# Weighted sums of an attention kernel as eight 64x32 TensorE tiles with two PSUM banks, and the single row maxima taken out of the main steps

## Chip, core and metric

The kernel runs on one core of one Trainium2 chip. The metric is the device time of one execution in microseconds (us): the median of the runs, 1456.09 us for the kernel before (2 runs, 1455.58 to 1456.61).

## What is computed

The reference mixes two attention branches of the same 2048 rows of x (512 wide) with a gate. All data are float32.

```python
x = A_x                                            # 2048 x 512
g = sigmoid((x * gate_w).sum(-1, keepdims=True))
# branch A: 32 heads of 16; each row sees 8 keys, 0, 2, ..., 14 rows back
# branch B: 32 query heads of 16, one key head and one value head for all of them
q = (x @ wq)  as 32 heads;  k = x @ wk;  v = x @ wv        # k, v: 2048 x 16
p = softmax(q k^T / 4);     o = p v                        # every row sees all 2048 keys
return g * a + (1 - g) * (o @ wo_b)
```

Branch B is the big part: 32 heads x 2048 queries x 2048 keys of scores, their exponentials, and the weighted sums of v.

## The kernel before, in words

**Units and steps.** Branch B is cut into 32 units: 4 blocks of 512 queries times 8 groups of 4 heads. A unit goes through 16 steps, one for each tile of 128 keys; all 512 steps stand in one loop (`for s in range(NS + 1)`). `kt` is the step's number in its unit. A step has these parts:

- `exp_pair(s, 0)` and `exp_pair(s, 1)` (L471, L477): TensorE computes two heads' scores of 128 keys x 512 queries into the two halves of a PSUM tile `pe0` or `pe1` (two matmuls that use the upper and the lower 64 rows of the array), and ScalarE writes their exponentials to an SBUF tile `pexp`.
- `weighted(s - 1)` (L486): the step before's `pexp` times `vst`, the values of the key tile (128 keys x 32 columns, of which 17 matter: 16 values and a column of ones, whose sum is the softmax's denominator). Head i of four goes to partitions 32i to 32i+31 of one PSUM bank, `po`, so four matmuls with 128x32 tiles of the array stand side by side. They add up over the 16 steps of a unit. These operands are full float32, and the profile shows each such matmul as two.
- Row maxima. The softmax needs each query's largest score ahead of its exponentials. They are found for units that come later, in 2048 pieces of 128 queries x 512 keys: TensorE computes the scores once more (L328), VectorE reduces them into `mx`. A **pair** (`fill_pair`, L350) does two pieces at once in a two-bank PSUM tile `pm`. A **single** (`fill_one`, L362) does one piece in the bank `m1`, which the profile calls `ps`. In the stages with other matmuls, `fill_diff` and `fill_sum` (L399, L411, L423) do two pieces with ScalarE's help.

When all 64 pieces of a unit are there, a chain makes two extra rows of that unit's query tile `qst` of them: L338 and L340 on VectorE, `mh` (L441) on ScalarE, `ml` (L447, L448) on GpSimd, eight small DMAs `qst<-ml` (L459). The unit's first score matmul waits for them.

**The order.** Each engine works its queue in program order. The program is written by a planner that runs at build time: it keeps clocks for the engines with fixed costs, and decides in each step which parts go in. `singles(s)` spreads singles over the steps so that the maxima are ready in time. Where a unit's maxima would come too late, `pause(n)` writes n pieces in a row, as pairs that take turns in `pe0`, `pm` and `pe1`, with no exponentials between them; the kernel before has no such pause.

**Unit end.** At a unit's end (`kt == 0` of the next) `finish_a` turns `po` on VectorE (L500), takes the reciprocals of the sums (L506), and GpSimd scales the result; the next unit's first weighted sum overwrites `po` and so waits for L500.

**Other stages.** Up to about 280 us the projections run (L1110, with maxima in between). GpSimd does branch A beside the main steps. Three times an output phase (`out_phase`, L804) computes four row groups of the output; there `m1` and `po` serve for maxima as well once the unit's sum has left `po`. The last rows of the output follow after step 511 (L1322, L1352); L1332 is the last unit's transpose.

Of the kernel before, what the change touches and what calls it, by code (L numbers as in the profile page):

```python
# [6 lines left out]
F32 = mybir.dt.float32  # L7
# [6 lines left out]
P = 128  # L14
S = 2048
D = 512
# [32 lines left out]
def gated_mix_kernel(ctx, tc, xt, wa, wk, wq, wo_a, wo_b, out):  # L49
# [280 lines left out]
    def to_go():  # L330
        return 2 * len(slots) + len(half)
# [151 lines left out]
    def weighted(s):  # L483
        u, kt = divmod(s, NJ)
        for i in (3, 2, 1, 0):
            nc.tensor.matmul(po[32 * i:32 * i + 32, :], vst[:, kt, :], pexp[s, i // 2][:, i % 2, :], start=(kt == 0), stop=(kt == NJ - 1))  # L486
        del pexp[s, 0], pexp[s, 1]
        after("pe", exped.pop(s) + 0.1, T_W)

# [7 lines left out]

    def finish_a(u, eng):
        tt = pe[0].tile([P, 4 * 4, 32], F32, name="tt", bufs=1)
        nc.vector.transpose(tt.rearrange("p b d -> p (b d)"), po)  # L500
        finish_b(u, tt, eng)

    def finish_b(u, tt, eng):
# [120 lines left out]
            woh.append(p2b[0].tile([P, C, D], F32R, name=f"woh{k}"))  # L624
            wol.append(p2b[0].tile([P, C, D], F32R, name=f"wol{k}"))

    wot = {}

    def wo_load(k, c):
        wot[k, c] = p2b[0].tile([P, 512], F32, name="os", tag="two", bufs=1)  # L630
# [2 lines left out]
    def wo_split(k, c):  # L633
        t = wot.pop((k, c))
        split(woh[k][:, c, :], wol[k][:, c, :], t, nc.gpsimd)

    turned, later = {}, {}

# [41 lines left out]
    def out_store(j, k, closing):  # L680
        nonlocal pool
        del turned[j, 0], turned[j, 1]
        two = p2b[0].tile([P, 2, D], F32, name="two", bufs=1)
        if closing:
            nc.scalar.activation(two[:, 0], eb[k][:, 0, :], AF.Copy)
            other = p2b[0].tile([P, D], F32, name="other", bufs=1)
            nc.vector.tensor_copy(other, eb[k][:, 1, :])  # L687
            free[f"e{k}"] = max(after("act", clk["pe"] + T_LAT, 0.5), after("dve", clk["pe"] + T_LAT, 0.66))
        else:
            nc.scalar.activation(two, eb[k], AF.Copy)  # L690
            free[f"e{k}"] = after("act", clk["pe"] + T_LAT, 0.92)
        pool = max(pool, 1e3 * free[f"e{k}"]) + 1300
        nc.gpsimd.tensor_add(two[:, 0], two[:, 0], other if closing else two[:, 1])
        nc.sync.dma_start(out[0].rearrange("(p j) d -> p j d", j=NJ)[:, j, :], two[:, 0])
# [47 lines left out]
    def stream(seq, mm, done, s):  # L742

        nonlocal pp2
        at, told = [0, 0], 0
        ready = free.pop("m2")
        pp2.release()
        pp2 = tc.alloc_tile_pool(name="parts", bufs=1, space=PSUM)
        if len(held[0]) < 2:
            more = p1x[0].tile([P, 2, 512], F32, name="dd2", tag="qx", bufs=1)  # L750
            for b in range(2):
                held[b].append(more[:, b])
                read_d[b].append(0.0)
        apart[:] = [pp2.tile([P, 512], F32, name=f"pd{k}") for k in range(2)]
        free["d0"] = free["d1"] = ready
        free["po"] = 1e9
        cl = [clk["pe"]] * 2
        while min(at) < len(seq) or any(pend):
            if free["po"] > 1e8 and min(at) > 3 and max(cl) > exped[s - 1] + 0.1:
                clk["pe"] = max(cl)  # L760
                weighted(s - 1)
                finish_a((s - 1) // NJ, nc.gpsimd)
                free["po"] = clk["dve"] + 0.1
                cl = [clk["pe"]] * 2
            if apart and max(at) > len(seq) - 10 and s in exped and max(free["d0"], free["d1"]) <= max(cl):
                clk["pe"] = max(cl)
                rejoin()
                exp_pair(s, 1, m2, "m2")
                cl = [clk["pe"]] * 2
            b = int(cl[1] < cl[0])  # L770
            clk["pe"] = cl[b]
            do = side_fill(b, max(at) > len(seq) - 10)
            if do:
                do()
                cl[b] += T_R
            elif at[b] < len(seq) and at[b] <= at[1 - b] + 2:
                dur = mm(b, seq[at[b]])
                cl[b] = clk["pe"] + dur
                at[b] += 1
            else:  # L780
                cl[b] += 0.07
            clk["pe"] = cl[b]
            while told < min(at):
                told += 1
                done(seq[told - 1])
        plain_todo()
        clk["pe"] = max(cl)
        if apart:
            rejoin()
            exp_pair(s, 1, m2, "m2")  # L790
# [79 lines left out]

    def singles(s):

        steps = 16 * (NU - 1) - 8 - s
        if steps <= 0 or to_go() <= 0:
            return to_go() > 0
        owing[0] += (to_go() - 1.94 * steps - 15.5 * (NJ - 4 - outs)) / steps
        owing[0] = min(owing[0], 3.0)
        if s % 16 == 1:
            return True
        if s % 16 == 0 or owing[0] < 1.0 or clk["dve"] - clk["pe"] > 1.5 and owing[0] < 2.0:  # L880
            return False
        return True

    def fill_ready(key, slack):
        if fillable() and free[key] <= clk["pe"] + slack:
# [375 lines left out]
    for s in range(NS + 1):  # L1261
# [18 lines left out]
        if outs == NJ - 4:  # L1280
            if short > 0 and steps < 2:
                pause(short)
        elif due or outs < NJ and outs // NH in done and kt == 15 and NHG * (k + 1) - 1 in shaped and (lead < LEAD or s >= 16 * (NHG * (k + 2) + 1) - 1):
# [44 lines left out]
    for x in range(2):  # L1328
        js = slice(2 * x, 2 * x + 2)
        two = four[:, x]  # L1330
        tt, own = two[:, 0].rearrange("p (b d) -> p b d", d=32), two[:, 1]
        nc.vector.transpose(two[:, 0], po[:, 256 * x:256 * x + 256])  # L1332
        rl = wp.tile([P, 8], F32, name="rll", tag="rl", bufs=2)
        nc.vector.reciprocal(rl, tt[:, :, 16])
        rv = rl.rearrange("p (j b) -> p j b", b=4)
        nc.vector.tensor_mul(rv, rv, gate_t[:, :, NJ - 4 + 2 * x:NJ - 2 + 2 * x].rearrange("p b j -> p j b"))
        nc.vector.tensor_mul(obp["t"][:, 8 * x:8 * x + 8, 1, :], tt[:, :, 0:DH], rl.unsqueeze(2).to_broadcast([P, 8, DH]))
        nc.vector.transpose(own, obp["t"][:, 8 * x:8 * x + 8].rearrange("p b h d -> p (b h d)"))
        tl = wp.tile([P, 2, 256], F32R, name=f"tl{x}", tag="aext", bufs=2)
# [53 lines left out]
```

## Time and profile before

| what | value |
|---|---|
| median of the runs | 1456.09 us |
| span of the profiled execution, first to last instruction | 1454.0 us |
| around the span (1456.09 - 1454.0) | 2.1 us |
| main steps with output phases | 282.4 us (first weighted sum) to 1432.5 us |
| granted TensorE clock | 1.00 throughout |

The profile's own execution has no time outside of its span, so the 2.1 us are the median's distance to it. The span is a sum of stages: projections to 280 us, then 512 steps, of which three hold an output phase of about 33 us, then some 21 us of last rows. Busy shares are means over all of them; what one step costs is read from the timeline.

### The profile page before, as it was taken

To read this page: it belongs to the slowest core of one execution; us is meant where nothing else is said; L and a number is where in the kernel's file an instruction comes from. 1 tells how busy PE (TensorE), PEld (TensorE's weight loads), DVE (VectorE), ACT (ScalarE), POOL (GpSimd) and SP (SyncE) were. 2 spreads that over 40 slices of the span, in tenths; PEclk is the share of its full clock that TensorE was granted. 3 is DMA by queue.
4 is the path that set the end of the run, shared out by engine and by line. 5 is a ranking of instruction groups with operands and counts; after the bars stand their busy time and mean duration, and the time that the engine had idled before them with its cause. 6 is when DMAs were issued, how large, how long until landed. Compare 5 with 4: busy or idle time off the path is not lost.

```text
span 1454.0 us, 29596 instructions
## 1 busy us (share of the span) xinstructions
PE 1445.0 (99%) x10989; PEld 744.9 (51%) x10989; DVE 1144.9 (79%) x1851; ACT 1289.6 (89%) x1643; POOL 955.1 (66%) x1716
## 2 busy tenths in 40 slices
PE   9999999999999999999999999999999999999999
PEld 6899999833333333333333373333333743373335
DVE  6888888788787888888888877888788778778821
ACT  5888888799999999999999979999999889879994
POOL 5941888888979898888898897988981211130000
PEclk9999999999999999999999999999999999999999
DMA  6652442411202102012022020211200000000000
GB/s 226 169 172 75 138 144 75 135 49 42 80 17 74 64 27 69 31 39 79 19 73 72 13 94 16 75 43 42 72 12 13 27 16 1 2 31 1 1 2 29
DMA packets 45688, 85.70 MB, mean 59 GB/s; under 512 B 10400, under 2 KB 28248, under 8 KB 41448
## 3 DMA queue, kind: packets, MB, share of 16 engines
q1 hardware_dynamic: 38552, 45.21, 10.1%
q0 software_dynamic: 6560, 37.95, 7.8%
q8 instruction: 86, 1.41, 0.4%
q10 hardware_dynamic: 432, 0.66, 0.1%
q14 instruction: 58, 0.48, 0.1%
HBM read 57.97 MB, written 25.25 MB: 57 GB/s over the span
## 4 chain that ended last, share of the span: by engine, by line
PE 96%; DVE 1%; ACT 1%; DMA 0%; issue 0%; POOL 0%; SPq 0%; ACTq 0%; DVEq 0%
PE po L486 34%; PE pe L471 25%; PE pf L1110 12%; PE pm L328 8%; PE ps L328 5%; PE pe L804 4%; PE pd L399 3%; PE po L328 1%; PE pe L1322 1%; PE pf L195 1%; ACT pexp L477 1%; DVE mx L350 1%; DMA xraw<-xt 0%; PE pm L862 0%; PE pe L652 0%
## 5 line engine op out<-in xcount | busy, mean ns | idle before, releaser
L477 ACT ACTIVATE pexp<-pe 128x1024 f32<-128x1024 f32 x1021 | 984.2, 1023 | 66.2 <-PE pe L471 61.9
L350 DVE TENSOR_REDUCE mx<-pm 128x2 f32<-128x1024 f32 x474 | 579.1, 1222 | 172.3 <-PE pm L328 168.9
L486 PE MATMUL po<-pexp,vst 128*32 128x512 f32 x4096 | 545.5, 605 | 0.0
L471 PE MATMUL pe<-qst,kst 64*128 64x512 f32 x1914 | 494.4, 458 | 3.3 <-DVE other L687 3.1
L471 PEld LDWEIGHTS pe<-qst,kst 64*128 64x128 f32 x1914 | 194.8, 183 | 437.5 <-ACT pexp L477 408.0
L411 ACT ACTIVATE dd<-pd 128x512 f32<-128x512 f32 x378 | 221.3, 602 | 50.6 <-PE pd L399 24.9
L362 DVE TENSOR_REDUCE mx<-ps 128x1 f32<-128x512 f32 x313 | 212.6, 679 | 4.4 <-PE pe L804 3.0
L328 PE MATMUL ps<-kst,qst 62*128 62x512 f32 x476 | 194.0, 408 | 0.1
L549 POOL TENSOR_TENSOR pr<-aext 128x256 f32<-128x256 f32 x256 | 182.0, 739 | 4.3 <-DMA aext<-ad 4.0
L328 PE MATMUL pm<-kst,qst 62*128 62x512 f32 x886 | 179.8, 398 | 0.3
L609 POOL TENSOR_TENSOR oa<-oa,av 128x256 f32<-128x256 f32 x224 | 164.2, 733 | 15.7
L486 PEld LDWEIGHTS po<-pexp,vst 128*32 128x32 f32 x4096 | 80.6, 108 | 167.8 <-issue 159.0
L423 DVE CUSTOM_DVE_ANT_0 dd<-ps,dd 128x512 f32<-128x512 f32 x190 | 130.9, 689 | 26.2 <-PE ps L328 10.5
L1110 PE MATMUL pf<-wah,xl 64*128 64x384 f32 (+1 forms) x496 | 149.2, 337 | 0.0
L606 POOL TENSOR_TENSOR av<-aext,lg 128x256 f32<-128x256 f32 x224 | 139.4, 622 | 12.8
L1110 PE MATMUL pf<-wah,xh 64*128 64x384 f32 (+1 forms) x496 | 147.4, 337 | 0.0
L1110 PE MATMUL pf<-wal,xh 64*128 64x384 f32 (+1 forms) x496 | 146.7, 337 | 0.0
L399 PE MATMUL pd<-kd,qst 62*128 62x512 f32 x366 | 144.3, 398 | 0.0
L423 DVE CUSTOM_DVE_ANT_0 dd<-po,dd 128x512 f32<-128x512 f32 x188 | 129.6, 690 | 17.9 <-PE po L328 8.8
L328 PEld LDWEIGHTS ps<-kst,qst 62*128 62x128 f32 x476 | 88.0, 185 | 33.0 <-DVE mx L362 27.1
L513 POOL TENSOR_TENSOR rl<-rl,gate_t 128x16 f32<-128x16 f32 x31 | 7.1, 230 | 136.6 <-DVE rl L506 136.5
L1110 PEld LDWEIGHTS pf<-wah,xl 64*128 64x128 f32 x496 | 91.1, 186 | 0.1
(211 smaller groups left out, 1816.1 us busy)
## 6 DMA issues: line engine op xcount, KB each, us to landing
aext<-ad POOLq DMA_DIRECT2D x32, 1056.0 KB, 5.5
ad<-stage SPq DMA_DIRECT2D x32, 384.0 KB
qst<-qd SPq DMA_DIRECT2D x60, 128.0 KB
xraw<-xt SPq DMA_DIRECT2D x16, 256.0 KB
qd<-qhi SPq DMA_DIRECT2D x16, 256.0 KB
qd<-qlo SPq DMA_DIRECT2D x16, 256.0 KB
qst<-qd SPq DMA_DIRECT2D x60, 64.0 KB
qst<-ml SPq DMA_DIRECT2D x212, 2.0 KB
```

The costliest lines, as they stand in the source:

```text
L328: nc.tensor.matmul(dst, qst[place(v)][b:b + 62, pr, t * P:(t + 1) * P], kst[b:b + 62, kc * 512:(kc + 1) * 512], start=True, stop=True)
L350: got = nc.vector.tensor_reduce(m[:, :, pr, t, kc], dst, AX.X, ALU.max)
L362: got = nc.vector.tensor_reduce(m[:, odd, pr, t, kc:kc + 1], dst, AX.X, ALU.max)
L399: nc.tensor.matmul(dst, qst[place(v)][b:b + 62, pr, t * P:(t + 1) * P], kd[0][b:b + 62, kc // 2, :], start=True, stop=True)
L411: got = nc.scalar.activation(held[b][k], dst, AF.Relu)
L423: got = nc.vector.tensor_tensor_reduce(held[b][k], dst, held[b][k], 1.0, -FMAX, ALU.add, ALU.max, m[:, b, pr, t, kc:kc + 1])
L471: nc.tensor.matmul(bank[:, odd, :], kst[b:b + 64, kt * P:(kt + 1) * P], qst[place(u)][b:b + 64, pr, :], start=True, stop=True)
L477: got = nc.scalar.activation(e, bank, AF.Exp, scale=SCALE)
L486: nc.tensor.matmul(po[32 * i:32 * i + 32, :], vst[:, kt, :], pexp[s, i // 2][:, i % 2, :], start=(kt == 0), stop=(kt == NJ - 1))
L549: nc.gpsimd.tensor_mul(pr[:, k], q, e[:, o:o + NH, AC:2 * AC])
L609: nc.gpsimd.tensor_add(ao, ao, av)
L1110: inst = nc.tensor.matmul(home(x)[0][:, :n], l[h], r[h], start=(i == 0 and b == 0), stop=(i == 3 * C - 1 and b == 1))
```

## The change

The weighted sum uses eight 64x32 tiles: keys 0 to 63 of a tile go to the bank `m1` (`ps`), keys 64 to 127 to `po`. At a unit's end ScalarE copies `m1` to a new SBUF tile `both`, VectorE adds `po`, and the transpose reads `both`. As `m1` is now taken during a unit, `singles` always says no. In an output phase `m1` is free for maxima only once the sum has left it. An output phase begins only when all of its weights are split. (Lines that only give a tile its tag or keep the list of splits are left out.)

```diff
     def weighted(s):
         u, kt = divmod(s, NJ)
         for i in (3, 2, 1, 0):
-            nc.tensor.matmul(po[32 * i:32 * i + 32, :], vst[:, kt, :], pexp[s, i // 2][:, i % 2, :], start=(kt == 0), stop=(kt == NJ - 1))
+            for b, bank in enumerate((m1, po)):
+                h = slice(64 * b, 64 * b + 64)
+                nc.tensor.matmul(bank[32 * i:32 * i + 32, :], vst[h, kt, :], pexp[s, i // 2][h, i % 2, :], start=(kt == 0), stop=(kt == NJ - 1))
...
     def finish_a(u, eng):
         tt = pe[0].tile([P, 4 * 4, 32], F32, name="tt", bufs=1)
-        nc.vector.transpose(tt.rearrange("p b d -> p (b d)"), po)
+        both = p2b[0].tile([P, 512], F32, name="both", tag="other", bufs=1)
+        nc.scalar.activation(both, m1, AF.Copy)
+        nc.vector.tensor_add(both, both, po)
+        nc.vector.transpose(tt.rearrange("p b d -> p (b d)"), both)
         finish_b(u, tt, eng)
...
-        free["po"] = 1e9
+        free["po"] = free["m1"] = 1e9
...
-                free["po"] = clk["dve"] + 0.1
+                free["po"] = free["m1"] = clk["dve"] + 0.1
...
     def singles(s):
 
-        steps = 16 * (NU - 1) - 8 - s
-        if steps <= 0 or to_go() <= 0:
-            return to_go() > 0
-        owing[0] += (to_go() - 1.94 * steps - 15.5 * (NJ - 4 - outs)) / steps
-        owing[0] = min(owing[0], 3.0)
-        if s % 16 == 1:
-            return True
-        if s % 16 == 0 or owing[0] < 1.0 or clk["dve"] - clk["pe"] > 1.5 and owing[0] < 2.0:
-            return False
-        return True
+        return False
...
-        elif due or outs < NJ and outs // NH in done and kt == 15 and ...
+        elif due or outs < NJ and not wot and len(split_done) == 2 * C and outs // NH in done and kt == 15 and ...
...
-        nc.vector.transpose(two[:, 0], po[:, 256 * x:256 * x + 256])
+        hs = slice(256 * x, 256 * x + 256)
+        if x == 0:
+            both = p2b[0].tile([P, 512], F32, name="both", tag="other", bufs=1)
+            nc.scalar.activation(both, m1, AF.Copy)
+            nc.vector.tensor_add(both, both, po)
+        nc.vector.transpose(two[:, 0], both[:, hs])
```

From here on the changed file's line numbers differ by a few: its weighted matmul is L488, its copy L503, its add L504, its transpose L505, its reciprocal L511.

**TensorE, an ordinary step** (step 359, `kt` 7 of unit 22). `pe_4203` and `pe_4204` are `pe0` and `pe1`; `ps` is the bank `m1`; `qst` with a number is a unit's query tile; `x2` means two equal rows. Before:

```order
L471 MATMUL pe_4203<-qst_80,kst 128x512 x2
L328 MATMUL pm<-kst,qst_82 128x512
L328 MATMUL ps<-kst,qst_76 128x512
L471 MATMUL pe_4204<-qst_80,kst 128x512 x2
L486 MATMUL po<-pexp,vst 32x512 x4
```

Now:

```order
L471 MATMUL pe_4203<-qst_80,kst 128x512 x2
L328 MATMUL pm<-kst,qst_81 128x512 x2
L471 MATMUL pe_4204<-qst_80,kst 128x512 x2
L488 MATMUL ps<-pexp,vst 32x512
L488 MATMUL po<-pexp,vst 32x512
L488 MATMUL ps<-pexp,vst 32x512
L488 MATMUL po<-pexp,vst 32x512
```

(The last two rows come twice more.) The single into `ps` is gone, and the four weighted matmuls are eight. Over the program the reductions of `ps` to one maximum go from 313 to 9. The query tile of the maxima is a sign of how far ahead they are: `qst_82` and `qst_76` belong to units 24 and 25 before, `qst_81` to unit 23 now, the very next one.

**TensorE, the next step** (step 360, `kt` 8 of unit 22). Before, it is the step above without the `ps` row. Now 17 pairs stand ahead of its exponentials, in turns of `pe_4203`, `pm` and `pe_4204`; these are the last four of them and what follows:

```order
L328 MATMUL pm<-kst,qst_81 128x512 x2
L328 MATMUL pe_4204<-kst,qst_81 128x512 x2
L328 MATMUL pe_4203<-kst,qst_81 128x512 x2
L328 MATMUL pm<-kst,qst_81 128x512 x2
L471 MATMUL pe_4203<-qst_80,kst 128x512 x2
L471 MATMUL pe_4204<-qst_80,kst 128x512 x2
L488 MATMUL ps<-pexp,vst 32x512
```

This is a pause. The program has 11 of them, at `kt` 8 of units 16, 20 to 24 and 26 to 30, with 159 pairs in all (10, 9 and 3 pairs at units 16, 20 and 26, and 17 or 18 at the other eight). Pairs in `pe0` and `pe1` go from 0 to 104, pairs in `pm` from 474 to 522. In the unit of a pause, `mh` of the next unit stands 4 steps ahead of that next unit on ScalarE (5 at the first pause); before, the shortest distance was 6 steps.

**VectorE at a unit's end.** Before:

```order
L340 STREAM_TRANSPOSE mt<-ms 128x32
L500 STREAM_TRANSPOSE tt<-po 128x512
L506 RECIPROCAL rl<-tt 128x16
L350 TENSOR_REDUCE mx<-pm 128x2
L362 TENSOR_REDUCE mx<-ps 128x1
```

Now:

```order
L504 TENSOR_TENSOR both<-both,po 128x512
L505 STREAM_TRANSPOSE tt<-both 128x512
L511 RECIPROCAL rl<-tt 128x16
L350 TENSOR_REDUCE mx<-pm 128x2 x2
L338 TENSOR_REDUCE ms<-mx 128x32
```

The add stands ahead of the transpose, and the next step's pair reduction behind all three. The copy that the add waits for stands on ScalarE behind the exponentials of the step in which the unit ends, and ahead of the next step's:

```order
L477 ACTIVATE pexp<-pe_4203 128x1024
L477 ACTIVATE pexp<-pe_4204 128x1024
L503 ACTIVATE both<-ps 128x512
L477 ACTIVATE pexp<-pe_4203 128x1024
L477 ACTIVATE pexp<-pe_4204 128x1024
```

Copy and add are there 31 times in the loop and once in the last rows. The output phases stand in steps 272, 288 and 400; before, in 272, 400 and 448.

More of the change, by code (lines that the diff above doesn't have):

```diff
@@ L625, in phase2 @@
             wol.append(p2b[0].tile([P, C, D], F32R, name=f"wol{k}"))
-    wot = {}
+    wot, split_done = {}, []
     def wo_load(k, c):
@@ L635, in wo_split @@
         split(woh[k][:, c, :], wol[k][:, c, :], t, nc.gpsimd)
+        split_done.append((k, c))
     turned, later = {}, {}
@@ L685, in out_store @@
             nc.scalar.activation(two[:, 0], eb[k][:, 0, :], AF.Copy)
-            other = p2b[0].tile([P, D], F32, name="other", bufs=1)
+            other = p2b[0].tile([P, D], F32, name="other", tag="other", bufs=1)
             nc.vector.tensor_copy(other, eb[k][:, 1, :])
@@ L1282, in gated_mix_kernel @@
                 pause(short)
-        elif due or outs < NJ and outs // NH in done and kt == 15 and NHG * (k + 1) - 1 in shaped and (lead < LEAD or s >= 16 * (NHG * (k + 2) + 1) - 1):
+        elif due or outs < NJ and not wot and len(split_done) == 2 * C and outs // NH in done and kt == 15 and NHG * (k + 1) - 1 in shaped and (lead < LEAD or s >= 16 * (NHG * (k + 2) + 1) - 1):
             if not due:
```

## Prediction

> **What bounds the kernel now.** I read the page first (busy shares and the chain of waits), then the timeline of two ordinary steps, then a unit's end.
>
> ```profile
> span 1454.0 us, 29596 instructions
> PE 1445.0 (99%) x10989; PEld 744.9 (51%) x10989; DVE 1144.9 (79%) x1851; ACT 1289.6 (89%) x1643; POOL 955.1 (66%) x1716
> PE 96%; DVE 1%; ACT 1%; DMA 0%; issue 0%; POOL 0%; SPq 0%; ACTq 0%; DVEq 0%
> ```
>
> TensorE holds 96% of the chain: nothing that it waits for is long, so what it issues, it pays for. ScalarE is next. The timeline of two steps shows how near it is (columns: start, length, engine, line, operation, shape, count):
>
> ```profile
> 699.46 1.94 ACT L477 ACTIVATE pexp<-pe 128x1024 f32<-128x1024 f32 x2 [0.19 <-PE pe L471]
> 699.69 1.23 DVE L350 TENSOR_REDUCE mx<-pm 128x2 f32<-128x1024 f32 x1
> 700.09 0.16 PEld L486 LDWEIGHTS po<-pexp,vst 128*32 128x32 f32 x8 [0.36 <-issue]
> 700.09 1.06 PE L486 MATMUL po<-pexp,vst 128*32 128x512 f32 x8
> 700.83 0.68 DVE L362 TENSOR_REDUCE mx<-ps 128x1 f32<-128x512 f32 x1
> 701.09 0.50 PE L471 MATMUL pe<-qst,kst 64*128 64x512 f32 x2
> 701.43 0.40 PE L328 MATMUL pm<-kst,qst 62*128 62x512 f32 x2
> 701.66 0.39 PE L471 MATMUL pe<-qst,kst 64*128 64x512 f32 x2
> 701.99 1.06 PE L486 MATMUL po<-pexp,vst 128*32 128x512 f32 x8
> ...
> 703.55 0.40 PE L328 MATMUL ps<-kst,qst 62*128 62x512 f32 x1
> 703.63 0.56 PE L471 MATMUL pe<-qst,kst 64*128 64x512 f32 x2
> ...
> 704.12 1.06 PE L486 MATMUL po<-pexp,vst 128*32 128x512 f32 x8
> ```
>
> From weighted sum to weighted sum a step without a single takes 701.99 - 700.09 = 1.90 us, one with a single 704.12 - 701.99 = 2.13 us: the single costs 0.23 us of TensorE, the distance at which matmuls of 512 columns follow each other (701.43 to 701.66). ScalarE's two exponentials fill 1.94 us; one alone takes 1.02 (row below), so the second starts 0.92 after the first, and a step cannot be shorter than 2 x 0.92 = 1.84 us whatever TensorE does. VectorE's pair reduction makes room for the next one after 700.83 - 699.69 = 1.14 us, well below a step.
>
> **The change, part by part.** The rows for the prices:
>
> ```profile
> L477 ACT ACTIVATE pexp<-pe 128x1024 f32<-128x1024 f32 x1021 | 984.2, 1023 | 66.2 <-PE pe L471 61.9 <-DVE mx L423 0.9
> L350 DVE TENSOR_REDUCE mx<-pm 128x2 f32<-128x1024 f32 x474 | 579.1, 1222 | 172.3 <-PE pm L328 168.9
> L486 PE MATMUL po<-pexp,vst 128*32 128x512 f32 x4096 | 545.5, 605 | 0.0
> L411 ACT ACTIVATE dd<-pd 128x512 f32<-128x512 f32 x378 | 221.3, 602 | 50.6 <-PE pd L399 24.9 <-DVE mx L423 13.3 <-PE pf L1110 2.1
> L663 DVE TENSOR_TENSOR qst<-pe,qst 128x512 fp32r<-128x512 f32 x12 | 8.2, 685 | 0.0
> ```
>
> *1. Singles out.* 313 become 9: 304 x 0.23 = **-70 us**. Hidden behind nothing, since TensorE is the bound of the step.
>
> *2. Their pieces come back in the pauses.* 159 pairs stand in 11 pauses. There TensorE has three places (`pe0`, `pm`, `pe1`), each free only when VectorE has read it, so VectorE sets the pace: 1.14 us a pair by the timeline, at most the 1.22 of the group's mean. No exponential can run beside them, since `pe0` and `pe1` hold maxima, so ScalarE's work cannot hide them. The next exponential needs the last turn but one, so a pause of n pairs holds the step up by n - 1 reductions: 159 - 11 = 148 x 1.14 = **+169 us** (to 148 x 1.22 = 181). The steps with a pause save their own pair, 11 x 0.23 = 2.5 us, which I leave for the start of each pause (a matmul before VectorE has anything to read).
>
> *3. The weighted sum itself.* As many products, on the same cells of the array: four tiles side by side of 128x32, or eight of 64x32. That two row halves run at once is seen: two 64-row matmuls take 0.39 (701.66), one 62-row matmul alone 0.40 (703.55). The eight loads of 108 ns take 0.16 us, so they follow each other after (160 - 108) / 7 = 7 ns; four more starts are 4 x 7 = 28 ns a step, 0.028 x 512 = **+14 us** (bounds: 0 if the halves start together, 28 if both passes pay). Nor do I count a gain from the shape. At 701.09 the score matmuls take 0.50, not 0.39, as their weights were not loaded ahead. The same happens where only the column width changes and the row count stays at 128:
>
> ```profile
> 1431.48 1.06 PE L486 MATMUL po<-pexp,vst 128*32 128x512 f32 x8
> ...
> 1432.48 0.19 PEld L1322 LDWEIGHTS pm<-woh,qst 128*128 128x128 f32 x1 [0.84 <-issue]
> 1432.48 0.50 PE L1322 MATMUL pm<-woh,qst 128*128 128x512 f32 x1
> ...
> 1432.81 0.39 PE L1322 MATMUL pe<-woh,qst 128*128 128x512 f32 x1
> ```
>
> The load sits idle for 0.84 us until the weighted sum is nearly through. So 32 columns against 128 suffice for the gap, and going from 64x32 to 64x128 should keep it.
>
> The Trainium skill says the same from another side: its page TensorEngine Tiling (Array Packing), section Tiling Modes, lists 64x32 and 64x128 as different configurations and says that changing the configuration drains the engine. By that rule the gap stays; if only the row count mattered, the sum would be that of the second rival below.
>
> *4. Unit ends.* Before, the transpose follows the sum, and the next weighted sum waits for it hardly at all:
>
> ```profile
> 345.94 3.84 ACT L477 ACTIVATE pexp<-pe 128x1024 f32<-128x1024 f32 x4 [0.19 <-PE pe L471]
> 346.31 1.06 PE L486 MATMUL po<-pexp,vst 128*32 128x512 f32 x8
> 347.50 0.72 DVE L500 STREAM_TRANSPOSE tt<-po 128x512 f32<-128x512 f32 x1
> 348.25 0.25 DVE L506 RECIPROCAL rl<-tt 128x16 f32<-128x16 f32 x1
> 348.42 1.16 DVE L350 TENSOR_REDUCE mx<-pm 128x2 f32<-128x1024 f32 x1
> 348.43 0.16 PEld L486 LDWEIGHTS po<-pexp,vst 128*32 128x32 f32 x8 [0.31 <-DVE tt L500]
> ```
>
> (That step has a single, so the transpose holds up little; at 1.90 a step without one would have the sum at 348.21.) Now ScalarE must first copy `ps`, behind the second of the four exponentials: its third starts about 345.94 + 2 x 0.92 = 347.78, so the copy (0.60 by L411) ends at 348.38. The add starts 0.13 later, as the transpose does behind the sum's end at 347.37, takes 0.69 (L663) and ends at 349.20; 0.21 later, as from the transpose's end at 348.22 to 348.43, the next sum may write `po`: 349.41, **1.20 us late**. Behind the add, VectorE still has the transpose 0.72, the reciprocal 0.25 and the pair reduction 1.16, to about 351.4. TensorE's next pair wants `pm` at 349.41 + 1.00 + 0.34 = 350.75 (700.09 to 701.09 to 701.43), and waits another 0.7. So 1.9 us at each of 31 - 3 = 28 ends outside the output phases: **+53 us** (bounds: only the first wait, with part of it hidden, 28 x 0.7 = 20; a reduction more in the way, 28 x 2.3 = 64). At the three in output phases `ps` also stays shut for copy and add: 3 x 1.3 = **+4 us** (0 to 8). The 32nd, in the last rows, adds 1.3 us behind this stretch of matmuls that need nothing of it, and would cost 1.3 without it:
>
> ```profile
> 1432.97 9.79 PE pe L1322 x42
> ```
>
> *5. The chain to the next unit.* In ten units `mh` now stands 4 steps ahead, 4 x 1.9 = 7.6 us. Before, the last unit's ran so:
>
> ```profile
> 1387.77 0.32 ACT L441 ACTIVATE mh<-mt,mk 128x32 fp32r<-128x32 f32 x1
> 1388.52 0.25 POOL L448 TENSOR_TENSOR ml<-mt,mh 128x32 fp32r<-128x32 f32 x1
> L459 SPq DMA_DIRECT2D qst<-ml x212: 599/611/768, 71.8 to 1390.8; - x106
> DMA to landing us min/median/max: 1.7/1.7/3.3
> ```
>
> With eight issues of 0.61 in one queue and 1.7 to land: 1388.77 + 4.9 + 1.7 = 1395.4, that is 7.6 us after `mh` began, just what there is; GpSimd's own work ahead of L447 comes on top while branch A lasts. **+5 us** (0 to 20). The later start of two output phases and the condition on the splits change only which step they follow: 0, since TensorE is busy in them either way.
>
> **Sum.** -70 + 169 + 14 + 53 + 4 + 5 = +175. The profiled execution spans 1454.0 us; the median of the runs is 2.1 above. 1454.0 + 175 + 2.1 = **1631 us**, 12% slower.
>
> **Rivals.**
> *Issue-bound (7%).* A step has 16 + 6 matmuls and as many loads, 44 rows against 28 now. If the engine cannot start more than it does in its densest long stretch, 2072 rows in 100 us or 48 ns each, a step takes 44 x 0.048 = 2.12 us: + 0.22 x 480 steps = 106, less term 3: 1631 + 106 - 14 = **1723 us**. For it: nothing denser lasts long. Against it: that stretch is made of other shapes with their own time, and short ones go at 0.33 / 16 = 21 ns.
>
> ```profile
> 100.00:200.00 100.00, 99.91 (x1036) 99.34 (x1036) 87.58 (x264) 86.03 (x179) 53.68 (x111) 1.00 0.36 114
> 1387.65 0.33 PEld L839 LDWEIGHTS pm<-ident,oa 64*128 64x128 f32 x8
> 1387.68 0.44 PE L839 MATMUL pm<-ident,oa 64*128 64x64 f32 x8
> ```
>
> The Trainium skill's page TensorE: Matmul & The Clock Gate (Part 1) has matmuls start no closer than about 25 ns; an estimate by that floor is 8 x 0.025 x 512 = 102 us for the eight more. The 7 ns above speak against it for tiles side by side.
>
> *No gap between shapes (9%).* If 64 rows before and after is enough, the weights are loaded ahead and ScalarE becomes the bound at 1.84: (1.90 - 1.84) x 480 = 29 us less, term 3 hidden, unit ends some 6 us less: 1631 - 29 - 14 - 6 = **1582 us**. Against it: the rows at 1432.48.
>
> *The row halves one after the other (4%).* The weighted sums would take up to their busy time again, 545.5 us by the row of L486: about **2176 us**. Against it: two halves at once at 701.66, though with another type of operand.
>
> *Pauses hidden (2%), not slower.* If the 148 reductions fell in time that TensorE waits anyway, term 2 would be 0: 1456.1 - 70 + 76 = **1462 us**. The point from which this decides: 2% above before is 1485, so a pair at under (1485 - 1462) / 148 = 0.16 us. For it, VectorE is only 79% busy; against it, TensorE's 99%, and that each reduction lasts 1.14 with three places to wait in.
>
> **How the numbers follow.** The forecast has 78%; with the bounds of its terms its own range is 1590 to 1665. For 8 in 10 I go down to take in the case without the gap, and up by as much as two terms that both miss; the issue-bound case, the row halves and the hidden pauses (13%) stay outside: 1560 to 1700. A measurement of this kernel tells about 2% from no change. Faster 1%; within 2%, the last rival, 2%; slower 97%.
>
> **What would show it.** Right: steps without a pause at 1.90 to 1.95; eleven stretches, eight of them near 20 us, with nothing but L328 and L350 and ScalarE idle; the weighted sum still near 1.1 us with the load idle ahead of the scores; a wait of about 1 us for L504 at each unit's end. Wrong: steps of 2.1 or at 1.84, a weighted sum near 2 us, or pairs in a pause closer than 1.1 us.

## The result, and the profile after

The changed kernel takes 1689.12 us (median of 2 runs, 1687.23 to 1691.0) against 1456.09 us: a ratio of 1.1603, 95% interval 1.1584 to 1.1622, so 16% slower. The prediction said 1631 us in a range of 1560 to 1700. The profiled execution spans 1685.4 us, 231.4 more than before.

The page of the changed kernel, with the rows that answer to those of before (engines, granted clock in 40 slices, chain, groups):

```profile
span 1685.4 us, 37813 instructions
PE 1567.0 (93%) x15084; PEld 756.0 (45%) x15084; DVE 1158.9 (69%) x1731; ACT 1310.2 (78%) x1678; POOL 956.3 (57%) x1719
...
PEclk9999999999999999999999999967977999777979
...
PE 30%; DVE 10%; issue 2%; ACT 2%; POOL 2%; DMA 1%; SPq 0%; DVEq 0%; POOLq 0%; ACTq 0%
...
L477 ACT ACTIVATE pexp<-pe 128x1024 f32<-128x1024 f32 x1021 | 990.3, 1025 | 276.0 <-PE pe L471 259.5
...
L350 DVE TENSOR_REDUCE mx<-pe 128x2 f32<-128x1024 f32 x104 | 122.8, 1219 | 7.2 <-PE pe L328 6.6
```

ScalarE does the same exponentials (990.3 us against 984.2), but sits idle 276.0 us ahead of them instead of 66.2, and 259.5 us of that end with scores (61.9 before). The chain could be followed over only half of the span (its shares add up to 47%), and in that half VectorE has gone from 1% to 10%: the reductions of the pauses, whose group `mx<-pe` is new. The granted clock, 1.00 throughout before, falls in the second half, where the pauses are.

Where the 231 us lie, from the starts of the weighted sums in the two traces (a step runs from one sum to the next; a unit's first step from its first sum to its second):

| stretch | before, us | after, us | difference | forecast |
|---|---|---|---|---|
| ordinary steps | 476 at 2.074 | 446 at 2.013 | 446 x -0.061 = -27 | -70 + 14 = -56 |
| 11 steps with a pause | none | 203.0 in all | 203.0 - 11 x 2.07 = +180 | +169 |
| 11 long steps right behind pauses | none | 37.7 in all | 37.7 - 11 x 2.07 = +15 | 0 |
| 8 long steps at the starts of units 21 to 24 | none | 40.0 in all | 40.0 - 8 x 2.07 = +23 | +5 (term 5) |
| first steps of the 32 units | 62.5 | 99.5 | +37 | +53 |
| 3 output phases | 99.3 | 102.8 | +3.5 | +4 |
| ahead of the first sum, from the last sum on | 282.4 + 22.5 | 281.9 + 23.0 | 0 | 0 |

**The ordinary step** of the changed kernel, in the timeline (TensorE's weight loads, score matmuls and the first load of each weighted sum):

```profile
488.24 0.10 PEld L488 LDWEIGHTS ps<-pexp,vst 64*32 64x32 f32 x1 [0.24 <-issue]
...
489.26 0.50 PE L471 MATMUL pe<-qst,kst 64*128 64x512 f32 x2
...
489.75 0.19 PEld L471 LDWEIGHTS pe<-qst,kst 64*128 64x128 f32 x2 [0.18 <-ACT pexp L477]
...
490.17 0.10 PEld L488 LDWEIGHTS ps<-pexp,vst 64*32 64x32 f32 x1 [0.24 <-issue]
...
491.19 0.19 PEld L471 LDWEIGHTS pe<-qst,kst 64*128 64x128 f32 x2 [0.84 <-ACT pexp L477]
...
491.80 0.19 PEld L471 LDWEIGHTS pe<-qst,kst 64*128 64x128 f32 x2 [0.30 <-ACT pexp L477]
...
492.23 0.10 PEld L488 LDWEIGHTS ps<-pexp,vst 64*32 64x32 f32 x1 [0.25 <-issue]
```

The eight-tile sum takes 489.26 - 488.24 = 1.02 us to the next scores, as the four-tile sum did (701.09 - 700.09 = 1.00), and the gap at the change of shape is still there (0.84 at 491.19). But the steps are 1.93 and 2.06 us, not 1.90. The second score pair of each step (489.75, 491.80) now waits 0.18 and 0.30 us for ScalarE to have read its place. The waits view sums it up, before and after (what waits, for what, us in total, times, longest):

```profile
PEld pe L471 <- ACT pexp L477: 435.0, 550, 1.1
```

```profile
PEld pe L471 <- ACT pexp L477: 494.3, 855, 1.7
...
PE pe L471 <- DMA qst<-ml: 16.1, 5, 4.5
```

550 rows have become 855, but they are of two kinds. By the single records, 504 of the 550 and 462 of the 855 stand right behind a weighted sum: they are the gap at the change of shape, with a median of 0.84 us in both kernels, and ScalarE did not end them: the exponential that is named had as a rule been over for 0.3 us or more (at 491.19 since 490.83). The other rows, nearly all ahead of the second score pair, are real waits for ScalarE, as they end 0.05 us behind its exponential. They go from 46 (12 us in all) to 393 (101 us). The row `qst<-ml` is the late chain of maxima, at unit starts.

**A unit's end** went as forecast, with smaller waits:

```profile
478.79 0.10 PEld L488 LDWEIGHTS ps<-pexp,vst 64*32 64x32 f32 x1 [0.25 <-issue]
...
480.11 0.61 ACT L503 ACTIVATE both<-ps 128x512 f32<-128x512 f32 x1
...
480.75 0.69 DVE L504 TENSOR_TENSOR both<-both,po 128x512 f32<-128x512 f32 x1 [1.00 <-ACT both L503]
480.77 0.13 PEld L488 LDWEIGHTS ps<-pexp,vst 64*32 64x32 f32 x2 [0.30 <-ACT both L503]
...
481.49 0.10 PEld L488 LDWEIGHTS po<-pexp,vst 64*32 64x32 f32 x1 [0.59 <-DVE both L504]
...
483.61 0.50 PE L328 MATMUL pm<-kst,qst 62*128 62x512 f32 x2 [0.60 <-DVE mx L350]
...
484.26 0.10 PEld L488 LDWEIGHTS ps<-pexp,vst 64*32 64x32 f32 x1 [0.36 <-issue]
```

Copy, add, then the sum into `po` 481.49 - 480.77 = 0.72 us behind the one into `ps`, and the pair of the next step 0.60 us late behind transpose, reciprocal and reduction. From sum to sum that is 484.26 - 480.77 = 3.49 us.

**The end of a pause** (9 pairs, unit 20; VectorE's reductions, the last scores on TensorE, ScalarE's exponentials):

```profile
1047.58 1.22 DVE L350 TENSOR_REDUCE mx<-pm 128x2 f32<-128x1024 f32 x1
...
1048.71 2.35 DVE L350 TENSOR_REDUCE mx<-pe 128x2 f32<-128x1024 f32 x2
...
1051.95 1.02 ACT L477 ACTIVATE pexp<-pe 128x1024 f32<-128x1024 f32 x1 [9.06 <-PE pe L471]
1052.10 1.22 DVE L350 TENSOR_REDUCE mx<-pe 128x2 f32<-128x1024 f32 x1
...
1053.37 0.80 PE L471 MATMUL pe<-qst,kst 64*128 64x512 f32 x2 [1.47 <-DVE mx L350]
...
1054.26 1.02 ACT L477 ACTIVATE pexp<-pe 128x1024 f32<-128x1024 f32 x1 [1.29 <-PE pe L471]
```

A reduction every 1.13 us (1047.58 to 1048.71), the forecast's 1.14. The first exponential comes early enough, but the second score pair of that step needs the place of the last reduction: the second exponential starts 1054.26 - 1051.95 = 2.31 us behind the first instead of 0.92. So it is in three of the eleven pauses (units 20, 21 and 26). In the other eight the last reduction is that of `pm`, and the two exponentials follow each other as usual, 1.94 us for both (unit 22, 17 pairs):

```profile
1174.79 1.94 ACT L477 ACTIVATE pexp<-pe 128x1024 f32<-128x1024 f32 x2 [19.29 <-PE pe L471]
```

### The profile page after: what moved, and what is told of

It is laid out like the page before. It is cut to its first block, busy times and chain, and to the rows that moved or that the text cites. A ratio compares the mean times of both kernels' runs of the same rounds, so it can differ in the third digit from the quotient of the medians.

```text
span 1685.4 us, 37813 instructions
## 1 busy us (share of the span) xinstructions
PE 1567.0 (93%) x15084; PEld 756.0 (45%) x15084; DVE 1158.9 (69%) x1731; ACT 1310.2 (78%) x1678; POOL 956.3 (57%) x1719
## 3 DMA queue, kind: packets, MB, share of 16 engines
q8 instruction: 118, 1.93, 0.5%
## 5 line engine op out<-in xcount | busy, mean ns | idle before, releaser
L477 ACT ACTIVATE pexp<-pe 128x1024 f32<-128x1024 f32 x1021 | 990.3, 1025 | 276.0 <-PE pe L471 259.5
L350 DVE TENSOR_REDUCE mx<-pm 128x2 f32<-128x1024 f32 x522 | 638.2, 1223 | 352.0 <-PE pm L328 350.4
L488 PE MATMUL ps<-pexp,vst 64*32 64x512 f32 x4096 | 586.1, 615 | 0.0
L488 PE MATMUL po<-pexp,vst 64*32 64x512 f32 x4096 | 568.2, 615 | 0.0
L471 PE MATMUL pe<-qst,kst 64*128 64x512 f32 x1914 | 465.1, 481 | 40.8 <-DVE mx L350 19.1
L471 PEld LDWEIGHTS pe<-qst,kst 64*128 64x128 f32 x1914 | 186.9, 190 | 529.4 <-ACT pexp L477 460.8
L328 PE MATMUL pm<-kst,qst 62*128 62x512 f32 x956 | 214.3, 440 | 31.0 <-DVE mx L350 31.0
L447 POOL TENSOR_TENSOR mt<-mt,mk 128x32 f32<-128x32 f32 x32 | 7.7, 240 | 290.6 <-ACT mh L441 276.6
L488 PEld LDWEIGHTS ps<-pexp,vst 64*32 64x32 f32 x4096 | 93.3, 106 | 143.6 <-issue 135.0
L328 PEld LDWEIGHTS pm<-kst,qst 62*128 62x128 f32 x956 | 96.5, 196 | 74.1 <-DVE mx L350 57.9
L350 DVE TENSOR_REDUCE mx<-pe 128x2 f32<-128x1024 f32 x104 | 122.8, 1219 | 7.2 <-PE pe L328 6.6
```

What stands on the lines that cost most here:

```text
L328: nc.tensor.matmul(dst, qst[place(v)][b:b + 62, pr, t * P:(t + 1) * P], kst[b:b + 62, kc * 512:(kc + 1) * 512], start=True, stop=True)
L350: got = nc.vector.tensor_reduce(m[:, :, pr, t, kc], dst, AX.X, ALU.max)
L471: nc.tensor.matmul(bank[:, odd, :], kst[b:b + 64, kt * P:(kt + 1) * P], qst[place(u)][b:b + 64, pr, :], start=True, stop=True)
L477: got = nc.scalar.activation(e, bank, AF.Exp, scale=SCALE)
L488: nc.tensor.matmul(bank[32 * i:32 * i + 32, :], vst[h, kt, :], pexp[s, i // 2][h, i % 2, :], start=(kt == 0), stop=(kt == NJ - 1))
```

## The experiments

**The eight tiles alone.** The changed kernel with four 128x32 tiles into `po` again, and the old unit end; pauses and missing singles stay.

```diff
-            for b, bank in enumerate((m1, po)):
-                h = slice(64 * b, 64 * b + 64)
-                nc.tensor.matmul(bank[32 * i:32 * i + 32, :], vst[h, kt, :], pexp[s, i // 2][h, i % 2, :], ...)
+            nc.tensor.matmul(po[32 * i:32 * i + 32, :], vst[:, kt, :], pexp[s, i // 2][:, i % 2, :], ...)
...
-        nc.vector.transpose(tt.rearrange("p b d -> p (b d)"), both)
+        nc.vector.transpose(tt.rearrange("p b d -> p (b d)"), po)
```

> The changed kernel's order, pauses included, with the weighted sum of before: four 128x32 tiles into one bank, and the old unit end without copy and add. The theory: in the changed kernel a step without a single takes 2.01 us instead of the 1.93 that was forecast because TensorE comes back to pe1 before ScalarE has read it; the tiles' shape has little to do with it. Then plain steps stay at 1.97 to 2.01, only the unit ends (32 x 1.16 = 37 us) and some 0.02 a step come off: 1635 to 1650 us. The rival: the shape itself costs 0.1 us a step. Then plain steps fall to 1.90 and the time to 1690 - 37 - 440 x 0.1 = about 1605 us.

Measured: 1645.3 us, ratio to before 1.1301 (1.1282 to 1.132); 1689.12 - 1645.3 = 44 us less than with the change whole. Over the 440 steps that are ordinary in both kernels the mean is 1.995 us (2.006 with eight tiles), the first steps of units take 2.00 us (3.11), the 11 steps with a pause 202.8 us (203.0). So the steps of 2.0 us aren't due to the shape: it costs about 0.01 us a step. The next run has eight tiles and the same unit end as this one, and takes 1650.31 - 1645.3 = 5 us more.

**The unit end alone.** The changed kernel without copy and add in the loop; the transpose reads `po`.

```diff
-        both = p2b[0].tile([P, 512], F32, name="both", tag="other", bufs=1)
-        nc.scalar.activation(both, m1, AF.Copy)
-        nc.vector.tensor_add(both, both, po)
-        nc.vector.transpose(tt.rearrange("p b d -> p (b d)"), both)
+        nc.vector.transpose(tt.rearrange("p b d -> p (b d)"), po)
```

> The changed kernel without the copy and the add at the 31 unit ends of the loop; the transpose reads po alone, so half of each weighted sum is left out of the output. The theory: a unit end costs 1.16 us more than before because the next weighted sum waits for copy and add, and the next pair for the transpose behind them: 32 x 1.16 = 37 us come off, 1648 to 1658 us. The rival: the unit end is late because ScalarE and VectorE are late there anyway; then under 15 us come off.

Measured: 1650.31 us, ratio 1.133 (1.1313 to 1.1347), 39 us less. The first steps of units fall from 3.11 to 2.02 us, and hardly anything else moves. The forecast had 53 + 4.

**The pauses alone.** The changed kernel; a pause counts its pairs as done without computing them.

```diff
...
-            fill_pair({"e0": eb[0], "e1": eb[1], "m2": m2}[key], key)
+            v, pr, t, kc = slots.pop(0)
+            unit_tile(v)
+            filled(v, 2)
```

> The changed kernel with the 159 pairs of the pauses left out (no matmul, no reduction; their maxima are missing, and mx begins at -1). The theory: the pauses cost 180 us by themselves, and another 31 us in the steps behind them (half clock, late chains): 1689 - 180 - 15 to 31 = 1478 to 1494 us, and a granted clock of 1.00. If the late chain has nothing to do with the pauses it stays, and 1494 is nearer. The rival: VectorE's time comes back elsewhere; then the time stays above 1530.

Measured: 1490.04 us, ratio 1.0231 (1.0211 to 1.0252): pauses, with the steps behind them, are 199 of the 233 us. The late starts of units 21 to 24 are not in the 199: the four steps that wait there take 5.65, 9.72, 6.02 and 6.10 us in this run, 27.5 in all as in the changed kernel. The mean granted clock is 0.993 against 0.941.

**The singles alone, in the kernel before.** Four tiles, one bank, no pauses; some 300 singles of the main steps are left out.

```diff
+        if pe and not apart and dst is m1:
+            free[key] = after("dve", after("pe", 0, T_R) + T_LAT, T_RED1) + 0.08
+            filled(v, 1)
+            return
         max_mm(dst, v, pr, t, kc, odd)
```

> The kernel before with the singles of its main steps left out (about 300 matmuls and reductions; those maxima are missing), everything else in the same order. By the prediction's price, 1.90 us a step without a single against 2.13, 300 x 0.23 = 69 us come off: about 1387 us. By the theory, steps in a row without singles cannot keep 1.90, since ScalarE then sets the pace together with the two places pe0 and pe1: they come to about 2.0, and 15 to 35 us come off: 1421 to 1441 us.

Measured: 1420.44 us, ratio 0.9754 (0.9739 to 0.9768). That is 36 us less, 0.12 us a single, and not the 70 of term 1. All ordinary steps are now without a single, and they take 1.989 us on average, not 1.90.

**What sets 2.0 us.** The same kernel without the pairs too: TensorE's ordinary step holds only scores and weighted sum.

```diff
     def fill_pair(dst, key):
         v, pr, t, kc = slots.pop(0)
         m = unit_tile(v)
+        if pe and not apart:
+            free[key] = after("dve", after("pe", 0, T_R) + T_LAT, T_RED2) + 0.08
+            filled(v, 2)
+            return
...
-        if pe and not apart and dst is m1:
+        if pe and not apart:
```

> The kernel before, with neither singles nor pairs in the main steps: their matmuls and reductions are left out and their maxima are set to a constant, so part of the computation is missing; the output phases are as they were. It asks what sets the 2.0 us of a step without a single. Theory: a loop of ScalarE and TensorE through the two places pe0 and pe1. The second score pair of a step cannot begin before ScalarE has read that place, 0.05 us behind the end of its exponential; from there 1.44 to the first score pair of the next step, 0.54 to its exponential, 0.92 and 1.03 to the end of the second, and so 3.98 us round for two steps. TensorE's maxima lie in the wait inside that loop, so without them a step stays at 1.95 to 2.0 us and the time at 1400 to 1422 us (1420.4 without the singles alone). Rival: TensorE's own work sets the step; then a pair less (0.33 us) brings it down to ScalarE's pace of 1.84 us, 450 steps x 0.15 = 68 us less, 1345 to 1370 us.

Measured: 1418.11 us, ratio 0.974 (0.9725 to 0.9754): only 2 us less than with the pairs. Ordinary steps take 1.993 us. Its timeline:

```profile
499.70 1.06 PE L494 MATMUL po<-pexp,vst 128*32 128x512 f32 x8
...
501.10 0.19 PEld L479 LDWEIGHTS pe<-qst,kst 64*128 64x128 f32 x2 [0.22 <-ACT pexp L485]
...
501.53 1.06 PE L494 MATMUL po<-pexp,vst 128*32 128x512 f32 x8
...
503.22 0.19 PEld L479 LDWEIGHTS pe<-qst,kst 64*128 64x128 f32 x2 [0.51 <-ACT pexp L485]
...
503.64 1.07 PE L494 MATMUL po<-pexp,vst 128*32 128x512 f32 x8
```

Two steps take 503.64 - 499.70 = 3.94 us, though TensorE has 0.33 us less to issue in each. The time has gone into the wait for ScalarE ahead of the second score pair (0.51 at 503.22). So TensorE's maxima don't set the step, and it is longer than ScalarE's pace of 1.84. What is left is a round through both engines, with two places for scores. In the changed kernel it can be followed in the single records of the trace: second scores' load 487.82, first scores of the next step 489.26 (+1.44), their exponential 489.80 (+0.54), the second one +0.92, its end +1.03, and 0.05 later the second scores' load at 491.80, two steps on: 3.98 us. That the two places make the round is read from these records; no run gives the scores a third place.

**Fewer changes of shape: two runs that missed.** The idea was that half of the gaps at a change of shape could be saved, in the kernel before, by doing the weighted sums of two steps in every second step.

```diff
...
+        owed.append((s, exped.pop(s)))
+        if s % 2 == 0:
+            return
+        for r, at in owed:
+            u, kt = divmod(r, NJ)
...
             for i in (3, 2, 1, 0):
-                nc.tensor.matmul(po[32 * i:32 * i + 32, :], vst[:, kt, :], pexp[s, i // 2][:, i % 2, :], ...)
+                nc.tensor.matmul(po[32 * i:32 * i + 32, :], vst[:, kt, :], pexp[r, i // 2][:, i % 2, :], ...)
```

> The kernel before (128x32 tiles, one bank, singles) with the weighted sums of two steps written one after the other in every second step, and a single allowed to wait 0.6 instead of 0.3 us of planner's time, so that no pause is needed; the output is the same. The theory: TensorE loses about 0.33 us at each change between 64x128 and 128x32 tiles and back; half of the changes gone is 0.16 us a step of 2.07, as far as ScalarE's pace (1.84 at least, 2.0 where nothing but its two places binds) lets it: 440 steps x 0.07 to 0.16, so 1386 to 1425 us. The rival: the two places pe0 and pe1 hold the pace at 2.0 to 2.1 whatever TensorE saves; then 1440 us or more.

Measured: 2011.78 us, ratio 1.3812 (1.3789 to 1.3835), a clear miss. The timeline shows one reason:

```profile
502.44 0.16 PEld L490 LDWEIGHTS po<-pexp,vst 128*32 128x32 f32 x8 [1.11 <-ACT pexp L477]
...
504.83 2.86 ACT L477 ACTIVATE pexp<-pe 128x1024 f32<-128x1024 f32 x3 [2.44 <-PE pe L471]
```

The weighted sum waits 1.11 us for an exponential in the midst of its matmuls, and ScalarE then 2.44 us for scores. The theory: the six places of `pexp` are taken in an order in which one exponential needs the place of a step whose sum has only just been issued. The second run tests it and takes the places in plain turn (the edit against the run before).

```diff
-        e = homes[len(homes) - 1 if turns[0] < 6 else (2 * (k % 3) + (y ^ k // 3 % 2) - 1) % 6]
+        e = homes[(turns[0] - 1) % 6]
```

> The kernel before with the weighted sums of two steps in every second step, as in the run before that missed, but the six places of the exponentials are taken in plain turn, so that no exponential waits for a sum that stands behind its own matmuls. If those places alone made the miss, the old expectation holds: half of the changes of tile shape are gone and the time is 1386 to 1425 us. The theory of the loop says otherwise: with both sums behind the second score pair of every second step, ScalarE has only two places of scores to work on for 2.1 us of sums, and then must wait for new scores. Round for two steps: first scores 0.54 to their exponential, 1.03 to its end, 0.05 to the next first scores, and so on: 2.97 to the next sums, and 2.06 for these: 5.0 us, or 2.5 a step against 2.07, 450 x 0.43 = 194 us more: 1620 to 1680 us.

Measured: 1681.64 us, ratio 1.1554 (1.1535 to 1.1574); 330 us of the miss were the places, but the rest stays, just above what the round foretold (1620 to 1680). Two steps of it:

```profile
502.18 0.16 PEld L489 LDWEIGHTS po<-pexp,vst 128*32 128x32 f32 x8 [0.25 <-issue]
...
504.63 3.92 ACT L476 ACTIVATE pexp<-pe 128x1024 f32<-128x1024 f32 x4 [0.91 <-PE pe L471]
...
505.71 0.19 PEld L471 LDWEIGHTS pe<-qst,kst 64*128 64x128 f32 x2 [0.92 <-ACT pexp L476]
...
507.35 0.16 PEld L489 LDWEIGHTS po<-pexp,vst 128*32 128x32 f32 x8 [0.37 <-issue]
```

507.35 - 502.18 = 5.17 us for two steps. Behind sums of 1.85 us (504.03 less 502.18) ScalarE has used up both places and waits 0.91 us; then TensorE waits 0.92 us for ScalarE. Half of the gaps are gone, and a step is 2.6 us long: a gap saved on TensorE is not time saved when ScalarE runs out of scores meanwhile.

**Half the clock.** In the pauses TensorE mostly waits, and the granted clock falls to 0.5. Here each pair of a pause is computed three times, so that TensorE is busier; nothing is left out.

```diff
...
-            fill_pair({"e0": eb[0], "e1": eb[1], "m2": m2}[key], key)
+            fill_pair({"e0": eb[0], "e1": eb[1], "m2": m2}[key], key, 3)
```

> The changed kernel with each pair of a pause computed three times over into the same place before VectorE reads it, so that TensorE is busy 0.7 us of each 1.2 instead of 0.23. The output is the same. The theory: TensorE is nearly idle in the pauses, its clock is halved in them and for some 10 us behind, and that makes the steps behind a pause last 3.3 to 3.5 us instead of 2.0 (8 x 1.4 = 11 us) and each pair of a pause 1.19 instead of 1.14 us (148 x 0.05 = 7 us). Then the granted clock goes to about 1.00 in the pauses and the time to 1668 to 1680 us. The rival: the extra matmuls only delay VectorE, and the slow steps come from waits; then 1689 us or more.

Measured: 1689.86 us, ratio 1.1607 (1.159 to 1.1624): no change, where 10 to 20 us less were expected, although the mean granted clock rose from 0.941 to 0.985. Stretches of the pause of 17 pairs in unit 22, the step behind it and what follows (stretch, length, busy time of each engine, granted clock, DMA share), changed kernel and then this run:

```profile
1154.10:1175.10 21.00, 13.63 (x56) 4.96 (x55) 20.25 (x18) 1.72 (x3) 10.59 (x20) 0.62 0.00 0
1175.10:1178.60 3.50, 3.50 (x30) 1.10 (x30) 0.78 (x1) 1.98 (x3) 0.00 (x0) 0.50 0.02 7
```

```profile
1158.80:1179.80 21.00, 17.57 (x124) 8.88 (x122) 19.86 (x18) 1.56 (x3) 10.73 (x20) 1.00 0.00 1
1179.80:1182.20 2.40, 2.40 (x28) 1.04 (x26) 0.79 (x2) 1.96 (x3) 0.00 (x0) 1.00 0.01 3
...
1509.60:1513.30 3.70, 3.70 (x28) 1.43 (x26) 0.55 (x2) 1.73 (x3) 0.00 (x0) 0.60 0.02 4
```

The pause itself takes 21.0 us at a clock of 0.62 and at 1.00, with its reductions 1.13 us apart in both: VectorE sets its pace. The step behind it takes 3.46 us at half clock and 2.38 at full, so there the low clock does cost 1.1 us. But only three pauses (units 22 to 24) gained from it: 3.46, 2.78 and 3.29 us became 2.38, 2.37 and 2.38. Behind the other pauses the clock still fell for 3.4 us, right where it costs (the last row is one: unit 28, 3.75 us where the changed kernel had 3.46). So this run doesn't tell what a full clock throughout would be worth; an estimate from the three units is at most 10 steps x 1.1 = 11 us.

**Pauses earlier.** The changed kernel with its pauses begun ten steps ahead of a unit instead of six.

```diff
-        steps = 16 * v - 6 - s
+        steps = 16 * v - 10 - s
```

> The changed kernel with the pauses four steps earlier in the unit (10 steps of margin instead of 6, so mh stands 8 or 9 steps ahead of its unit instead of 4). As many pairs in pauses. The theory: in the units 21 to 24 the first step waits 3 to 5.5 us for the small DMAs behind mh and ml; with the margin these waits go, some 15 to 20 us: 1668 to 1676 us. The rival: the long steps at these unit starts are the clock's or the copy's doing; then the time stays within 5 us of 1689.

Measured: 1674.29 us, ratio 1.1498 (1.1481 to 1.1515), 15 us less. No step outside of pauses and output phases is longer than 3.6 us; four unit starts had been at 7.31, 7.39, 7.55 and 5.22. Its steps with a pause take 209.1 us instead of 203.0, so some 6 us of what the waits gave back went there.

**Why the chain was late.** The order in SyncE's queue at unit 21, with the landing ahead of the scores (changed kernel):

```profile
1061.72 3.33 SPq L459 DMA_DIRECT2D qst<-ml  x5
1067.53 0.60 SPq L296 DMA_DIRECT2D qst<-qd  x1
...
1069.46 0.57 SPq L297 DMA_DIRECT2D qst<-qd  x1
1070.08 2.02 SPq L459 DMA_DIRECT2D qst<-ml  x3
```

```profile
1074.00 1.94 ACT L477 ACTIVATE pexp<-pe 128x1024 f32<-128x1024 f32 x2 [5.10 <-PE pe L471]
```

Five of the unit's eight small DMAs go out, then four loads of the unit after next stand in the queue. They write over the query tile of the unit that is ending, so they wait for its last scores (to 1067.53). The last three small DMAs stand behind them, and the new unit's scores wait for these. To test it, the eight are given to the queue closer together, so that all stand ahead of the loads. The pauses stay, with 157 pairs instead of 159, and `mh` stands 5 steps ahead of units 21 to 25 instead of 4.

```diff
-            tasks.append((clk["pe"] + (1.2 if pe else 0.8) * k, shift_d, (v, ml, k)))
+            tasks.append((clk["pe"] + (0.3 if pe else 0.8) * k, shift_d, (v, ml, k)))
```

> The changed kernel whole, except that a unit's eight small DMAs from ml are given to the queues close together, so that in SyncE's queue all eight stand ahead of the four loads of the unit after next; in the changed kernel three of the eight stand behind these loads at units 21 to 24. The pauses stay (157 pairs), and mh stands 4 steps ahead at units 27 to 31 as before and 5 instead of 4 at units 21 to 25. Theory: the waits of 5.3, 5.4, 5.5 and 3.2 us at the start of units 21 to 24 come from the queue: the four loads write over the query tile of the unit that ends, so they wait for its last score matmuls, and the three last small DMAs wait behind them. With the order mended the waits are gone: 1689 - 19 = 1670 us, with what follows them 1666 to 1676 us. Rival: four steps are too few for the chain itself (mh, ml, eight issues of 0.61 us and the landing); then one step more buys at most 2 us at each of these units and the time stays at 1681 to 1690 us.

Measured: 1665.82 us, ratio 1.1435 (1.1415 to 1.1456), 23 us less. Now the queue reads, for the same unit:

```profile
1061.78 5.30 SPq L459 DMA_DIRECT2D qst<-ml  x8
```

and units 21 to 24 begin without a wait: their first steps are 3.5 us like other units' ends, and the steps ahead of them ordinary ones. So it was in the main the order in the queue. The one step more of lead that came with it was not tested alone; by the forecast of this run it is worth at most 2 us at each of these units. None of the runs with all of the computation beats the kernel before.

## Why the prediction came out where it did

The sign and the main mechanism were right: the pauses carry the loss (199 us by the run without them, ratio 1.0231 left). The sum was 58 us short. With the bounds of its own terms it reached 1665 us, so 1689 lies in the range only by the margin that was added for terms that miss together. That the margin was enough is in part luck, since one term missed the other way. Its own sign of being right, steps of 1.90 to 1.95 us, did not come.

- **Term 1, singles out (-70), with term 3 (+14).** The failed step is "Hidden behind nothing, since TensorE is the bound of the step". The two steps were read rightly, 1.90 us without and 2.13 with a single. But the 1.90 was that of a step behind one with a single: the longer step gives ScalarE the time to catch up, and the next one profits. Two such steps take 2.13 + 1.90 = 4.03 us, a round without any single 3.98. With all singles gone a step is 1.99 (1.993 without pairs too). The singles were worth 36 us and not 70; the two terms together came to -27 instead of -56. The sign was in the trace of before: its 144 steps without a single behind a step with one have a mean of 1.90 us, its 31 behind another without one 2.01. TensorE's 96% of the chain did not show it; the prediction took it to mean that whatever TensorE no longer issues is saved.
- **The shape.** 5 us instead of 14, about 0.010 us a step instead of 0.028; the row halves do run at once. The gap stayed, as the row at 491.19 shows. By the rule on drains (the Trainium skill, TensorEngine Tiling (Array Packing), section Tiling Modes) it should, and the trace agrees with it for 64x32 to 64x128: 0.84 us idle. The rival without the gap fell at this row, the issue-bound one at the steps of 2.0 us, the same with four tiles and with eight, the one with the row halves in turn at the eight-tile sum of 1.02 us, and the one with hidden pauses at the 199 us.
- **Term 2, pauses (+169).** The price was right, 1.13 us a pair against 1.14: 148 x 1.13 = 167. The rest of the 180, 13 us, is what the starts and ends of the eleven pauses cost beyond n - 1 reductions: 0.9 us at each of the seven pauses of 17 pairs, 1.3 to 2.4 at the other four. "The next exponential needs the last turn but one" fails at three of these four (units 20, 21 and 26), where the second score pair needs the last place and its exponential starts 1.39 us late. At the others the cause was not told apart.
- **Term 4, unit ends (+53).** Mechanism right, waits too large: 0.72 and 0.60 us instead of 1.20 and 0.7. The copy ended sooner (480.72, 1.93 us behind the start of the sum at 478.79, against 2.07), and beside steps of 2.0 us less of it shows. Measured were +37 in the trace and 39 us by the run without copy and add. Output phases: +3.5, forecast +4.
- **Term 5, the chain (+5).** "eight issues of 0.61 in one queue" counted what the chain issues, but not what stands between them in SyncE's queue. The waits cost 5.3, 5.4, 5.5 and 3.2 us at four units (19), the eight steps there 23 us, and the run with the order mended is 23 us faster.
- **The step behind a pause** was no term of the sum: ten steps of 2.8 to 3.5 us (one of 5.2, with a second long one behind it), about 1.4 us too long each, 15 us in all. Up to 1.1 of the 1.4 is the half clock; the rest was not told apart.

The differences, 29 (ordinary steps) + 11 (pauses) + 15 (behind them) + 18 (chain) - 16 (unit ends and output phases) + 1.6 (the median lies 3.7 above the profiled span, not 2.1), make the 58 us to within 1. The runs that take one part away each give the same account: 199 (pauses) + 39 (unit ends) + 23 (queue) + 5 (shape) - 36 (singles, measured in the kernel before) = 230 of the 233 us.

## What to carry to other kernels

A step's time that is read beside steps of another kind is not its time among its like: go round the loop of engines and places once (here 3.98 us for two steps), and average over all steps that have like neighbours, before a saving on a busy engine is taken as time. A row of the waits view can mix two kinds of idle time under one name; sort the single records by what stands ahead of them. Work that is moved into a pause costs the slowest engine's pace there plus the refilling of the pipeline behind it. When a chain moves nearer to its deadline, read the whole queue that its DMAs go through in order, and ask what each entry ahead of them waits for.

## What the runs showed of the hardware that was not expected

- The granted clock fell to 0.5 in the pauses, for some us behind them and at the late starts of units 21 to 24, 199 us in all ((1 - 0.941) x 1685.4 / 0.5). Inside the pauses it cost nothing that shows (21.0 us at 0.62 and, with three times the matmuls, at 1.00); in the step behind a pause up to 1.1 us. The Trainium skill (TensorE: Matmul & The Clock Gate, section Terms) puts the penalty at about the throttled time x (1 - K/N), with K/N the share of the clock that is granted; an estimate by it is 199 x 0.5 = 99 us. The rows of the pauses speak against that where another engine sets the pace.
